# Threshold attention with an MLP behind it: two W transposes moved from TensorE to DMA, the w_out load moved later, one q copy moved up

## The chip, the cores and the metric

The kernel runs on one core of a Trainium2 chip, in one launch. The metric is the device time of that launch in microseconds (us). The kernel before took 495.15 us (median of three runs: 494.38, 495.15 and 495.28).

## The reference

Eight batches of eight heads attend over 576 tokens with 64 dimensions per head. Of each row of scores only those within tau = 0.02 of the row's largest are kept. The attention's output, 4608 tokens of 512 numbers, goes through an MLP with a leaky ReLU.

```python
scores = scale * np.matmul(q, k.transpose(0, 1, 3, 2))          # scale = 1/8
thresh = np.max(scores, axis=-1, keepdims=True) - tau
scores = np.where(scores >= thresh, scores, -1000000000.0)
attn = np.exp(scores - np.max(scores, axis=-1, keepdims=True))
attn = attn / (np.sum(attn, axis=-1, keepdims=True) + 1e-09)
x = np.matmul(attn, v)                                          # heads side by side: 4608 x 512
h = x @ w_in                                                    # 512 x 2048
out = np.maximum(0.01 * h, h) @ w_out                           # 2048 x 512
```

## The kernel before, in words

**Steps.** The work is cut into 144 steps, 18 for each batch. A step takes 128 queries of one pair of heads; the two last steps of a batch take the 64 left-over queries of all heads. Two steps that follow each other (c = 0 and c = 1) make a *pair*: their weights W lie side by side in one tile `w` (`Pair`, line 300). Steps 0 and 1 are the first pair, 4 and 5 the third, 6 and 7 the fourth. The first four pairs give the first 256 tokens of the MLP's input `x`.

**What a step does.** TensorE multiplies q and k (`scores`, L252). The numbers are split in a high and a low half of 16 bits, so a score is three products. VectorE copies the scores out of PSUM, negates them and takes the row's minimum on the way (`copy_min`, L260; two instructions, one per head), then the threshold (`threshold`, L269 in the first 28 steps). ScalarE makes the exponentials (`exps`, L295, L291, L292) one step later, and VectorE the masked weights of the first head (`weights`, L304). The reciprocal of the row sums (`recip`, L310) is written beside the weights by `widen` (L313), so that it is transposed with them.

**The transpose of W.** W must have the keys on the partitions before it can be multiplied with v. There are two ways. `turn_w_pe` (L331, L333) does it in two halves of 10 TensorE transposes for each step, with copies out of PSUM by ScalarE (three of a pair's four) and VectorE (one). `turn_w` (L321) does it for a whole pair with one transposing DMA from the SP queue. `Step.early` (line 34) decides: steps below 8 go by TensorE, two steps behind their scores. All later pairs go by DMA: the pair is noted in `ended` at the end of a step, and in the next step VectorE takes the reciprocal, GpSimd widens it, and SP issues the DMA.

**W times v.** `pv` (L348) follows at a fixed step given by `pv_at`: three steps after the pair's second step for early pairs, five for the others. `evacuate` (L370, VectorE) multiplies by the reciprocal and puts the result into `x`. After the fourth pair of heads `x` is complete, and eight pieces of the first MLP layer (`layer1`, L391) are queued, one of which goes into each later step; the second layer (`layer2`, L407) follows, up to two pieces a step.

**q and k.** They come by DMA from HBM, are scaled and split (`split_*`, L137, L143, L151, mostly on GpSimd) and transposed by TensorE (`turn`, L186) with a copy out of PSUM (L195, L189). The keys of the first batch are in the list `first`; `first[8]` is the last head pair's q, which `scores` first needs in step 6, and `first[9]` the tail's q.

**Order.** There is no scheduler: each engine runs its instructions in the order in which the Python loop writes them, and waits where a tile isn't ready. In a step the order is: loads, `exps` of the step before, `scores`, `copy_min`, the reciprocal of a noted pair, idle products in the first steps, one item of the list for GpSimd (`pool_at`), `threshold`, `widen` and `turn_w` of a noted pair, the rest of `pool_at`, `weights` of the step before, `layer1`, `turn`, `turn_w_pe`, `layer2`, idle products in steps 5 to 10, `pv` and `evacuate`. The SP queue holds the loads of q, k and v, the transposing DMAs and the stores, in the order of the steps. The loads of w_in and w_out are issued by GpSimd (`load_w`, L497 and L500), on a DMA queue of their own, and convert to 16 bits on the way.

**Idle products.** `idle` (L513) multiplies the identity with itself into the PSUM tile of `pv`; nothing reads the result. Since that tile has one buffer, idle products wait for the `evacuate` before them.

**Buffers that matter here.** PSUM: scores two buffers for each head, `pv` one, the "h" tag two. SBUF: `w` three, transposed `wT` four, raw q and k four.

Of the kernel before, what the change touches and what calls it, by code (L numbers as in the profile page):

```python
# [16 lines left out]
class Group:  # L17


    def __init__(self, tokens, where):  # L20
        self.tokens = tokens
        self.where = where
        self.x = None
        self.g = None


class Step:


    def __init__(self, n, b, blk, p, c):  # L30
        self.n, self.b, self.blk, self.p, self.c = n, b, blk, p, c
        self.tail = blk == 2

        self.early = n < 8


@with_exitstack
def kernel(
# [10 lines left out]
    nc = tc.nc  # L49
# [68 lines left out]
    def turned_of(b, which):  # L118
        if (b, which) not in turned:
            turned[b, which] = sb.tile([128, 2, NP, WIDE[which]], FP16, tag=f"{which}T", bufs=2, name=f"{which}T")  # L120
        return turned[b, which]
# [23 lines left out]
    def split_low(key):  # L145

        n = 2 if key[1] == "t" else 4
        m = 2 if key[0] < 2 else n
        src = scaled.pop(key)
        for i in range(0, n, m):  # L150
            nc.gpsimd.tensor_tensor(out=halves[key][:, 1, i : i + m, :, :], in0=src[:, i : i + m, :, :],  # L151
                                    in1=halves[key][:, 0, i : i + m, :, :], op=AX.subtract)
# [18 lines left out]
    def turn(key, copy=None, bank="h"):  # L171
        copy = copy or nc.scalar.copy
        b, p, which = key
        dst, half = turned_of(b, which), halves.pop(key)
        n = 2 if p == "t" else 4
        c0 = 0 if which == "q" else 64
        if p == "t":
            c0 = MAIN if which == "q" else 0
            tp = ps.tile([128, 2, 2, 2, 64], FP16, tag=bank, bufs=2 if bank == "h" else 1, name="tp")
        else:  # L180
            tp = ps.tile([128, 2, 4, 128], FP16, tag="h", bufs=2, name="tp")
        for x in range(2):
            for t in range(n):
                for h in range(2):
                    o = tp[ds(64 * h, 64), x, :, t, :] if p == "t" else tp[ds(64 * h, 64), x, t, :]
                    nc.tensor.transpose(o, half[:, x, t, h, :], ident[:, :])  # L186
        if p == "t":
            src = tp[:, :, :, :, :].rearrange("d x u s p -> d x (u s) p")
            copy(out=dst[:, :, :, ds(c0, 64)], in_=src)  # L189
            if which == "k" and b:  # L190
                nc.gpsimd.tensor_copy(out=dst[:, :, :, 576:640], in_=dst[:, :, :, 0:64])
            elif which == "k":
                nc.vector.tensor_copy(out=dst[:, :, :, 576:640], in_=src)
        else:
            copy(out=dst[:, :, p, ds(c0, 512)], in_=tp[:, :, :, :].rearrange("d x t p -> d x (t p)"))  # L195
# [31 lines left out]
    steps = []  # L227
# [9 lines left out]
    def scores(st):  # L237
        st.sc = [ps.tile([128, 2, 512], FP32, tag="sc", bufs=2, name=f"sc{h}") for h in range(2)]
        for kh in range(2):
            for i, (qx, kx) in enumerate(((0, 0), (1, 0), (0, 1))):  # L240
                for u in range(2 if st.tail else 1):
                    for h in range(2):
                        pair = st.p + u
                        rows = ds(64 * h, 64)
                        key0 = 64 * (1 - h) + 288 * kh
                        if st.tail:
                            lhs = turned[st.b, "q"][rows, qx, pair, MAIN:S]
                            o = st.sc[h][ds(64 * u, 64), kh, 0:288]
                        else:
                            lhs = turned[st.b, "q"][rows, qx, pair, ds(256 * st.blk + 128 * st.c, 128)]  # L250
                            o = st.sc[h][:, kh, 0:288]
                        nc.tensor.matmul(out=o, lhsT=lhs, rhs=turned[st.b, "k"][rows, kx, pair, ds(key0, 288)],  # L252
                                         start=(i == 0), stop=(i == 2), skip_group_check=True)
# [54 lines left out]
    def recip(pr, c, n):  # L308
        pr.rec = sb.tile([128, 2, 2], FP32, tag="rec", bufs=2, name="rec")
        nc.vector.reciprocal(out=pr.rec[:, 0:n, :], in_=pr.sum[:, ds(c, n), :])  # L310

    def widen(pr, c, n, eng=None):
        (eng or nc.gpsimd).tensor_copy(out=pr.w[:, ds(c, n), 9, :].rearrange("q c (h d) -> q c h d", h=2),  # L313
                                     in_=pr.rec[:, 0:n, :].unsqueeze(3).to_broadcast([128, n, 2, 64]))
# [114 lines left out]
    loads_at, turns_at, pool_at = {}, {}, {}  # L429

    def at(d, n, f):
        d.setdefault(n, []).append(f)

    def units(b):
        u = [(b, p, w_) for p in range(NP) for w_ in "kq"]
        return u[:2] + [(b, "t", "k")] + u[2:] + [(b, "t", "q")]
# [3 lines left out]
    for b in range(1, B):  # L440
# [6 lines left out]
        for i, key in enumerate(units(b) if b == 1 else ROWS):  # L447
            n_ = 9 + 3 * i // 2 if b == 1 else base + (5, 7, 9, 9, 11, 13, 15, 17, 19, 21)[i]
            key = (b,) + key[-2:]
# [45 lines left out]
    def load_w(i):  # L495
        if i < 4:
            nc.gpsimd.dma_start(out=w_in16[:, i, :], in_=moe_w_in[ts(i, 128), :])  # L497
        else:
            j = i - 4
            nc.gpsimd.dma_start(out=w_out16[:, ds(4 * j, 4), :],  # L500
                                in_=moe_w_out[ds(512 * j, 512), :].rearrange("(j p) f -> p j f", p=128))


    def split_pool(key):
        split_scale(key)
        split_high(key)
        split_low(key)
# [8 lines left out]
    first = units(0)  # L516
# [8 lines left out]
    for key in first[4:6]:  # L525
        split_high_act(key)
        split_scale(key)
        split_low(key)
    for n_, key in zip((1, 2, 6), first[7:]):
        at(pool_at, n_, lambda key=key: split_pool(key))  # L530
    for i in range(8):
        at(pool_at, i if i < 2 else 1 + i // 2 if i < 6 else i, lambda i=i: load_w(i))
    at(turns_at, 0, lambda: turn(first[3], nc.vector.tensor_copy))
    for n_, key in zip((1, 2, 3, 5, 8), first[5:]):
        at(turns_at, n_, lambda key=key: turn(key, nc.vector.tensor_copy if key[2] == "q" else None))

    N = len(steps)

    pv_at = {s.n + (3 if s.early else 5): s for s in steps if s.c == 1}
    ended = []  # L540
    n = 0
    while n < N + 7 or l1q or l2q or stores:
        for f in loads_at.get(n, []):
            f()
        if 1 <= n <= N:
            exps(steps[n - 1])
        if n < N:
            scores(steps[n])
            turned_now = turn_rows(rows_at[n]) if n in rows_at else None
            copy_min(steps[n])  # L550
            if ended:
                recip(ended[0], 0, 2)
        if n == 0:
            threshold(steps[0])
        if n == 1:
            split_high_act(first[6])
            split_scale(first[6])
            split_low(first[6])
            turn(first[4], nc.vector.tensor_copy)
        if n < 5:  # L560
            idle(8 if n else 16)
        todo = pool_at.get(n, [])
        for f in todo[:1]:
            f()
        if 0 < n < N:
            threshold(steps[n])
        if ended:
            widen(ended[0], 0, 2)
            turn_w(ended.pop())
        if n in rows_at:  # L570
            turned_now(1)
        for f in todo[1:]:
            f()
        if 1 <= n <= N:
            last = steps[n - 1]
            weights(last)
            if last.early:
                recip(last.pair, last.c, 1)
                widen(last.pair, last.c, 1, nc.vector if n < 7 else nc.gpsimd)
            elif last.c == 1 and n < 2 * PERB:  # L580

                ended.append(last.pair)
            elif last.c == 1:
                recip(last.pair, 0, last.pair.n)
                widen(last.pair, 0, last.pair.n)
                turn_w(last.pair)
        if n in rows_at:
            turned_now(0)
        while stores:
            store()  # L590
        if l1q and l1q[0][3] <= n:
            layer1()
        for f in turns_at.get(n, []):
            f()
        if 2 <= n < N + 2 and steps[n - 2].early:
            turn_w_pe(steps[n - 2].pair, steps[n - 2].c)
        for _ in range(2):
            if l2q:
                layer2(n)
        if 5 <= n < 11:  # L600
            idle(8)
        if n in pv_at:
            pv(pv_at[n])
            evacuate(pv_at[n], n)
        n += 1
# [33 lines left out]
```

## Time and profile before

| | us |
|---|---|
| median of three runs | 495.15 |
| the profiled execution | 495.05 |
| its span, from the first to the last instruction | 493.2 |
| TensorE busy | 476.3 |
| ScalarE busy | 431.3 |
| VectorE busy | 408.8 |
| GpSimd busy | 316.3 |
| start of step 6's first `copy_min` | 30.68 |
| start of step 12's first `copy_min` | 50.16 |
| start of step 18's first `copy_min` | 67.94 |

The profiled execution's own time is 1.85 us above its span. A time in the trace counts from the span's start. A convenient mark for "where a step is" is the start of the first of its two L260 instructions on VectorE; the table gives three of them. The engines' busy times overlap, and a share over the whole span hides stages: the first 68 us, in which the MLP has not filled up, look different from the rest. "PEclk" is the TensorE clock that was granted, 1.00 being full. A DMA line gives the packets, the megabytes and the share of time of the 16 DMA engines in the window asked for; q1 is the queue of the DMAs that SP issues, q0 that of GpSimd's.

### The profile page before, as it was taken

What the parts mean: (1) busy time and instruction counts of PE and PEld (TensorE: products, weight loads), DVE (VectorE), ACT (ScalarE), POOL (GpSimd) and SP (SyncE); (2) the same over time, 40 slices, a digit from 0 to 9 for tenths busy, and PEclk for the clock granted to TensorE, in tenths of its full rate; (3) what the DMA queues carried; (4) which work ended last, traced back from release to release, by engine and by line L of the source; (5) the groups of instructions that cost most, each with busy time, mean ns of one, the idle gap of its engine ahead of it and who ended that gap; (6) DMA issues with size and microseconds to landing.
All of it is one profiled execution on the core that took longest, in us unless ns stands there. A gap on an engine that the chain in (4) does not pass through costs nothing.

```text
span 493.2 us, 19697 instructions
## 1 busy us (share of the span) xinstructions
PE 476.3 (97%) x8039; PEld 344.5 (70%) x8039; DVE 408.8 (83%) x1220; ACT 431.3 (87%) x781; POOL 316.3 (64%) x534
## 2 busy tenths in 40 slices
PE   8978989999999999999999999999999999999996
PEld 7656766767677777777777777777777777667883
DVE  4989999998989898989889898989889998888100
ACT  6889988999999999999999999999999999999441
POOL 5996798578766786768766787677767683222000
PEclk9989999999999999999999999999999999999999
DMA  8998799989998998999997898999999988769412
GB/s 247 263 205 144 140 185 186 210 176 192 212 185 160 221 208 196 180 174 234 166 209 162 201 211 198 192 165 224 179 202 163 205 134 169 125 128 146 113 45 66
DMA packets 220443, 87.79 MB, mean 178 GB/s; under 512 B 190656, under 2 KB 217280, under 8 KB 220352
## 3 DMA queue, kind: packets, MB, share of 16 engines
q1 hardware_dynamic: 217120, 82.00, 82.4%
q0 software_dynamic: 2688, 4.19, 4.8%
q8 instruction: 63, 1.03, 0.9%
q10 hardware_dynamic: 544, 0.33, 0.2%
q14 instruction: 28, 0.23, 0.1%
HBM read 36.70 MB, written 9.44 MB: 94 GB/s over the span
## 4 chain that ended last, share of the span: by engine, by line
PE 82%; DVE 4%; ACT 1%; issue 1%; DVEq 0%
PE hp L391 27%; PE o L407 21%; PE sc L252 21%; PE pv L348 7%; PE osc L407 4%; PE tpr L207 3%; DVE s L260 2%; DVE w L304 1%; DVE x L370 0%; PE tp L186 0%; ACT w L292 0%; ACT s L291 0%; ACT e L295 0%; ACT g L393 0%; ACT osb L413 0%
## 5 line engine op out<-in xcount | busy, mean ns | idle before, releaser
L260 DVE TENSOR_SCALAR_CACHE_REDUCE s<-sc 128x576 f32<-128x576 f32 x288 | 206.5, 754 | 34.5 <-PE sc L252 33.0
L252 PE MATMUL sc<-kT,qT 64*128 64x288 f16 (+1 forms) x1920 | 135.1, 285 | 5.2 <-DVE s L260 2.5
L391 PE MATMUL hp<-x,win 128*64 128x256 f16 x2048 | 136.7, 275 | 0.8 <-DVE x L370 0.7
L391 PEld LDWEIGHTS <-win 128*64 128x64 f16 x2560 | 118.5, 109 | 23.8 <-issue 17.8
L407 PE MATMUL o<-wout,g 128*64 128x512 f16 x992 | 127.8, 379 | 0.0
L304 DVE SCALAR_TENSOR_TENSOR w<-s,th,e 128x576 f16<-128x576 f32 x144 | 120.5, 837 | 0.5 <-ACT e L295 0.5
L272 POOL TENSOR_SCALAR th<-mn 128x2 f32<-128x2 f32 x116 | 53.7, 463 | 102.1 <-DVE s L260 79.1
L252 PEld LDWEIGHTS <-qT 64*128 64x128 f16 (+1 forms) x1920 | 76.6, 96 | 59.4 <-issue 42.7
L292 ACT ACTIVATE w<-s,minus_tau 128x576 f16<-128x576 f32 x144 | 111.7, 775 | 5.2
L295 ACT ACTIVATE e<-s,mn 128x576 f16<-128x576 f32 x144 | 110.2, 765 | 2.0 <-DVE s L260 2.0
L291 ACT ACTIVATE s<-s,th 128x576 f32<-128x576 f32 x144 | 110.3, 766 | 1.3 <-POOL th L272 0.9
L393 ACT ACTIVATE g<-hp 128x512 f16<-128x512 f32 x144 | 84.0, 584 | 26.9 <-PE hp L391 26.4
L151 POOL TENSOR_TENSOR half<-scaled,half 128x512 f16<-128x512 f32 (+1 forms) x91 | 90.2, 998 | 2.0
L407 PEld LDWEIGHTS <-g 128*64 128x64 f16 x1152 | 65.2, 110 | 30.0 <-issue 0.5
L348 PE MATMUL pv<-wT,v 128*64 128x256 f16 (+1 forms) x960 | 52.6, 249 | 1.0 <-DMA wT<-w 0.8
L348 PEld LDWEIGHTS <-v 128*64 128x64 f16 x960 | 42.2, 111 | 14.5 <-issue 1.0
L137 POOL TENSOR_SCALAR scaled<-raw 128x512 f32<-128x512 f32 x62 | 44.3, 714 | 5.7 <-DMA raw<-in_k_dram 4.8
L143 POOL CAST half<-scaled 128x512 f16<-128x512 f32 (+1 forms) x74 | 44.3, 599 | 4.5
L313 POOL CAST w<-rec 128x256 f16<-128x256 f32 (+1 forms) x70 | 32.1, 459 | 15.9 <-DVE rec L310 4.6
L106 POOL CAST v<-vraw 128x256 f16<-128x256 f32 x64 | 31.3, 520 | 1.3
L370 DVE TENSOR_TENSOR x<-pv,wT 128x256 f16<-128x256 f32 x64 | 27.0, 422 | 3.8 <-PE pv L348 3.6
L292 ACT ACTIVATION_READ_ACCUMULATOR w<-s,minus_tau 128x1 f32 x144 | 26.9, 187 | 0.0
(53 smaller groups left out, 323.9 us busy)
## 6 DMA issues: line engine op xcount, KB each, us to landing
vraw<-in_v_dram SPq DMA_DIRECT2D x16, 512.0 KB, 5.8
out_dram<-osb SPq DMA_DIRECT2D x16, 512.0 KB, 3.7
raw<-in_k_dram SPq DMA_DIRECT2D x14, 512.0 KB, 4.9
raw<-in_q_dram SPq DMA_DIRECT2D x14, 512.0 KB, 4.9
win<-in_moe_w_in_dram POOLq DMA_DIRECT2D x4, 512.0 KB, 7.1
wout<-in_moe_w_out_dram POOLq DMA_DIRECT2D x4, 512.0 KB, 10.3
wT<-w SPq DMA_TRANSPOSE x68, 5.7
raw<-in_k_dram SPq DMA_DIRECT2D x4, 256.0 KB, 5.3
```

The source lines that it names most:

```text
L151: nc.gpsimd.tensor_tensor(out=halves[key][:, 1, i : i + m, :, :], in0=src[:, i : i + m, :, :], in1=halves[key][:, 0, i : i + m, :, :], op= ...
L252: nc.tensor.matmul(out=o, lhsT=lhs, rhs=turned[st.b, "k"][rows, kx, pair, ds(key0, 288)], start=(i == 0), stop=(i == 2), skip_group_check= ...
L260: nc.vector.tensor_scalar(out=st.s[:, h, :].rearrange("p (a b) -> p a b", a=2), in0=st.sc[h][:, :, 0:288], scalar1=-1.0 / UNIT, scalar2=No ...
L272: nc.gpsimd.tensor_scalar(out=st.th[:, :, 0], in0=st.mn[:, :, 0], scalar1=1.0, scalar2=tau_f, op0=AX.mult, op1=AX.add)
L291: nc.scalar.activation(out=z, in_=z, func=AF.Prelu, bias=st.th[:, h, 0:1], scale=-1.0, alpha=1e20)
L292: nc.scalar.activation(out=st.w[h], in_=z, func=AF.Exp, bias=minus_tau[:, :], scale=1.0, accum_out=st.sum[h])
L295: nc.scalar.activation(out=st.e[:, :], in_=st.s[:, h, :], func=AF.Exp, bias=st.mn[:, h, 0:1], scale=-1.0)
L304: nc.vector.scalar_tensor_tensor(out=st.w[0], in0=st.s[:, 0, :], scalar=st.th[:, 0, 0:1], in1=st.e[:, :], op0=AX.is_le, op1=AX.mult, accum ...
L348: nc.tensor.matmul(out=o, lhsT=v16[st.b % 2][:, 2 * c + u if st.tail else st.p, blk, :], rhs=rhs, start=(i == 0), stop=(i == 4), skip_grou ...
L391: nc.tensor.matmul(out=hp[ds(64 * u2, 64), jj, :], lhsT=w_in16[:, i, ds(128 * j + 64 * u2, 64)], rhs=g.x[:, i, :], start=(i == 0), stop=(i ...
L393: nc.scalar.activation(out=g.g[:, ds(nj * u, nj), :], in_=hp[:, :, :], func=AF.Prelu, bias=0.0, scale=1.0, alpha=0.01)
L407: nc.tensor.matmul(out=g.o[ds(64 * u2, 64), :], lhsT=g.g[:, j, ds(128 * m + 64 * u2, 64)], rhs=w_out16[:, j, :], start=(j == 0), stop=(j = ...
```

## The change

The third and the fourth pair's W go by DMA, with `pv` four steps behind the pair's second step (at steps 9 and 11, where it was at 8 and 10). Their reciprocals are taken for the pair as a whole, by one instruction of VectorE and one `widen` on GpSimd, at steps 7 and 9. The four pieces of w_in stay at steps 0, 1, 2 and 2; the four pieces of w_out move from steps 3, 3, 6 and 7 to steps 8, 9, 10 and 11. The copy of the last head pair's q (and its transposes, which already came right behind the scores on TensorE) is written directly behind `copy_min` of step 5, where it stood at that step's end. The tail's q is split at step 7 and turned at step 10, where it was 6 and 8. The number of idle products stays 96 in steps 0 to 10; in steps 6, 8 and 10 they move from the end of the step to behind the scores.

```diff
-        self.early = n < 8
+        self.early = n < 4
...
-    for n_, key in zip((1, 2, 6), first[7:]):
+    for n_, key in zip((1, 2, 7), first[7:]):
         at(pool_at, n_, lambda key=key: split_pool(key))
     for i in range(8):
-        at(pool_at, i if i < 2 else 1 + i // 2 if i < 6 else i, lambda i=i: load_w(i))
+        at(pool_at, i if i < 2 else 2 if i < 4 else 4 + i, lambda i=i: load_w(i))
...
-    for n_, key in zip((1, 2, 3, 5, 8), first[5:]):
+    for n_, key in zip((1, 2, 3, 10), first[5:8] + first[9:]):
...
-    pv_at = {s.n + (3 if s.early else 5): s for s in steps if s.c == 1}
+    pv_at = {s.n + (3 if s.early else 4 if s.n < 8 else 5): s for s in steps if s.c == 1}
...
             copy_min(steps[n])
             if ended:
                 recip(ended[0], 0, 2)
+            if n == 5:
+                turn(first[8], nc.vector.tensor_copy)
...
-        if n < 5:
+        if n < 11 and (n < 5 or n % 2 == 0):
             idle(8 if n else 16)
...
-                widen(last.pair, last.c, 1, nc.vector if n < 7 else nc.gpsimd)
+                widen(last.pair, last.c, 1, nc.vector)
...
-        if 5 <= n < 11:
+        if 5 <= n < 11 and n % 2:
             idle(8)
```

On the SP queue the two new DMAs stand ahead of loads that were issued early: the third pair's ahead of the second half of the next batch's k and q (`load_main` of steps 8 and 9), the fourth pair's behind these two and ahead of the first v load of the next batch (step 11).

## The prediction

> **What bounds the kernel now.** I read first the page, then the windows by stage, then the timeline around step 6, then the DMA queues in short windows.
>
> From the page:
>
> ```profile
> PE 476.3 (97%) x8039; PEld 344.5 (70%) x8039; DVE 408.8 (83%) x1220; ACT 431.3 (87%) x781; POOL 316.3 (64%) x534
> PEclk9989999999999999999999999999999999999999
> ```
>
> TensorE (PE) is the bound on average. The dip of the clock is a hint that the first tenth is different. Stages, with the columns span length, then busy time and count of PE, weight loads, VectorE (DVE), ScalarE (ACT), GpSimd (POOL), then granted clock, DMA share, GB/s:
>
> ```profile
> 26.04:30.68 4.64, 2.29 (x48) 1.69 (x50) 3.47 (x13) 4.57 (x9) 4.64 (x11) 1.00 0.89 185
> 30.95:34.36 3.41, 3.35 (x38) 2.48 (x34) 3.20 (x12) 3.05 (x7) 3.20 (x6) 0.50 1.00 191
> 30.68:50.16 19.48, 17.50 (x282) 12.85 (x283) 18.14 (x62) 16.91 (x31) 15.32 (x23) 0.91 0.89 161
> 50.16:67.94 17.78, 15.15 (x274) 11.78 (x272) 17.50 (x57) 16.86 (x32) 15.01 (x24) 1.00 0.81 158
> 65.08:68.49 3.41, 1.96 (x28) 1.50 (x29) 3.25 (x11) 2.85 (x7) 3.26 (x6) 1.00 0.56 118
> 67.94:100.00 32.06, 31.35 (x524) 22.26 (x522) 31.18 (x105) 28.26 (x51) 23.89 (x37) 1.00 1.03 198
> 100.00:450.00 350.00, 349.15 (x5962) 249.33 (x5960) 313.57 (x911) 325.87 (x596) 235.80 (x400) 1.00 0.93 184
> ```
>
> From step 18 (67.94) PE is busy 98% and then 99.8%: there the time is PE's work, which the change doesn't shorten. All it touches lies before that. From step 6 to step 18 VectorE is the bound (18.14 of 19.48, 17.50 of 17.78). So the end moves by as much as step 18 moves, plus PE work that changes sides of that point. Before step 6 stands a hole:
>
> ```profile
> 29.00 0.68 DVE L195 COPY qT<-tp 128x1024 f16<-128x1024 f16 x1
> 29.74 0.91 PE L252 MATMUL sc<-kT,qT 64*128 64x288 f16 x12 [2.35 <-DVE qT L195]
> 30.68 0.76 DVE L260 TENSOR_SCALAR_CACHE_REDUCE s<-sc 128x576 f32<-128x576 f32 x1 [1.00 <-PE sc L252]
> 50.27 3.15 SPq L321 DMA_TRANSPOSE wT<-w  x1
> 57.01 0.74 PE L348 MATMUL pv<-wT,v 128*64 128x256 f16 x10 [0.84 <-DMA wT<-w]
> 58.70 0.76 DVE L260 TENSOR_SCALAR_CACHE_REDUCE s<-sc 128x576 f32<-128x576 f32 x1
> ```
>
> Step 6's scores wait 2.35 us for the q copy, VectorE then 1.00 us for the scores, and from 30.95 the clock is halved for 3.41 us (window above). The last three lines are the first transposing DMA: though pv comes five steps behind, PE waits for it. DMA in short windows: both queues at 34 to 37, w_out alone at 38 to 45, that first transpose alone at 51.2 to 54.9, and the landing of eleven transposes:
>
> ```profile
> q0 software_dynamic: 339, 0.35, 70.4%
> q1 hardware_dynamic: 341, 0.35, 42.1%
> ...
> q0 software_dynamic: 1434, 1.43, 123.6%
> ...
> q1 hardware_dynamic: 2592, 0.66, 94.7%
> ...
> wT<-w SPq DMA_TRANSPOSE x1, 6.7
> ...
> DMA to landing us min/median/max: 4.9/5.5/7.2
> ```
>
> So a piece of w_out (0.52 MB) is 2.5 us of all DMA engines, a transpose about 3.1 us, and where GpSimd's queue and SP's both have work, neither goes first: they share packet by packet.
>
> **The change part by part.** Marks are the starts of a step's first L260.
>
> A. The q copy behind step 5's scores. It goes in at 27.50, where the threshold stood, ends at 28.2, and step 6's scores start at 28.25 in place of 29.74. With 0.94 from scores to L260 (29.74 to 30.68) step 6 starts at 29.2. Threshold and weights come 0.7 later and still end by then. Gain 1.5.
>
> B. VectorE's work in steps 6 to 11. A step with nothing but scores, threshold, weights and one pair's reciprocal took 2.53 (47.63 to 50.16). Six make 15.2; three evacuations (start to start 0.33) 1.0; two 128x1024 copies (0.60) 1.2; the tail's q copy 0.3. Sum 17.7 against 19.48: gone are two L333 copies (481 ns), three small reciprocals (168), a widen (227), 1.34 of idle time, and the halved clock, whose cause A removes. PE's 80 transposes (0.72 for 20, 2.9 in all) and ScalarE's six copies (690, 4.1) lie beside VectorE and count nothing; without that cover they would be up to 2.9 more gain. Gain 1.8. Without any wait step 12 would start at 46.9 in place of 50.16.
>
> C. The third pair's transpose. Step 7 starts at 29.2 + 2.53 + 0.33 = 32.1; reciprocal 1.35 later (47.63 to 48.98); from there to SP's issue 1.3 (48.98 to 50.27): 34.7. The landing took 4.9 at best and 6.7 for the kernel's first transpose, which this one now is, with the DMA as empty as there; I take 6.7, 41.4. From pv's start to the next L260 it was 1.69 (57.01 to 58.70): step 10 starts at 43.1, against 40.6 by VectorE alone. Loss 2.5 (0.7 at 4.9). PE stands behind that pv with step 10's scores.
>
> D. The fourth pair's. Its reciprocal is at 38.5 (step 9 at 37.1), but GpSimd has before that widen one scale, one high half and one low half of q, the same of the tail's q, a further scale and the first w_out issue: by the rows 615, 829, two of 747, 398, about 400, 720, 398 and 825 ns, 5.7 after 34.7. Then widen: SP issues at 41.1. In its queue stand two 0.52 MB loads that were issued at 17.5 and 23.4 before and now wait behind C's issue, till 37.9 and 38.5 (1.5 us of DMA each); beside them w_out pieces from about 40.5, one each 2 to 3 us. With equal shares the loads end near 43.3, the transpose needs 2 x 3.1, and lands at 50.2 (0.7 behind its last packet). Step 12 starts at 51.9, against 43.1 + 3.45 + 2.86 = 49.4 without this wait. Loss 2.5. Bounds: 0 (it lands in 5.0 at 46.1, and 47.8 is below 49.4), and 8 if the transpose's 2592 packets alternate one to one with w_out's. I take the equal share, from the row with both queues, 339 against 341.
>
> By the Trainium skill, "DMA: Bandwidth & Descriptors", section on queues, rings and completion order, an engine changes queue only at packet borders, of typically 9 to 17 descriptors; the row of 339 and 341 has pieces of equal size and can't show which of the two counts. By that rule a transpose's pieces of 256 B would hold their half (D = 2.5); by the row read one to one it would be 8.
>
> The moved loads and vector v of batch 1 are not needed before step 12; w_out is needed at step 19 and has 20 us. GpSimd loses two narrow widens and gets two wide ones (292 against 464 ns), which cancels but for 0.3.
>
> E. The clock. In D PE waits from about 45 to 50: longer than the 2.35 that halved it. In a halved window pv took 1.28 for 0.74, scores 1.17 for 0.91 (rows at 32.57 and 33.78). Loss 1.0 (0 if D is 0, 1.5 for a whole window). Steps 7 and 8 now have 0.91 + 0.62 of PE work in 2.5 us, 61%; 57% (1.96 of 3.41 at 65.08) passed without halving, 35% (1.21 of 3.41 at 27.54) did not. The moved idle products cost nothing while PE waits for VectorE anyway; were one late, it would be 0.62.
>
> By the Trainium skill, "TensorE: Matmul & The Clock Gate", the table of why this matters, only idle gaps above about 3 us cool the clock. The gap of 2.35 here did, in a window with 35% of work; by that rule C's gap of about 2 us would be harmless, by the row it could add up to 1.5.
>
> F. `layer1` starts a step later, so one piece (16 products, 0.99) leaves the part that VectorE bounds and joins the part that PE bounds. 0 to 1.0; VectorE is 97% busy in 67.94 to 100, so half: 0.5.
>
> Sum: -1.5 - 1.8 + 2.5 + 2.5 + 1.0 + 0.5 = +3.2. The profiled execution, 495.05 (0.1 below the median of the runs, so no correction), becomes 498.3.
>
> **The rivals.** R1, the transposes land in time. For it: from 33 to 36 the DMA now has nothing, 4.9 us is a common landing, and C then costs 0.7 and D and E nothing: -3.3 + 0.7 + 0.5 = -2.1, 492.9. Against it: the one transpose of before that met an empty DMA is the 6.7. It decides when C's transpose lands before 40 and D's before 47.5.
>
> R2, the first lands late and the second is hidden behind it (D and E 0): -3.3 + 2.5 + 0.5 = -0.3, 494.8, no difference. For it: C itself gives D time. Against: GpSimd's 5.7 us and the loads in front are in no row faster.
>
> R3, w_out gets a packet for each of the transpose's: D = 8, E = 1.5: 504.3. For it: 339 to 341. Against: nothing shows it for 256-byte pieces.
>
> That the change does nothing at all I leave out: the 2.35 us hole goes in any case, since PE's transposes of that q end at 26.27 and only VectorE's order kept the copy back.
>
> **How the numbers follow.** Forecast 0.50, R1 0.28, R2 0.12, R3 0.10. What a measurement of this kernel can tell from no change is about 0.2%, 1 us. Faster 0.28, same 0.12, slower 0.60. Predicted 498.3. The range takes in R1 with another 0.4 for F at nothing, and reaches up to half way into R3: 492.5 to 502.0; the forecast's own is 496 to 502.
>
> **What would show it.** A: no PE wait for qT before step 6, step 6 at about 29.2. B: steps 7 and 8 of about 2.5. C: a PE wait of pv for the DMA near 39 to 41. D: another near 45 to 50, the fourth pair's landing over 8 us after its issue, both DMA queues busy together. E: a row of granted clock 0.50 behind that wait, none at 31. F: PE full from step 18 or 19 on. The prediction is wrong if the DMA serves the transpose ahead of w_out, if GpSimd reaches its widen earlier, or if steps 12 to 18 give back what was lost.

## The result

The changed kernel takes 508.83 us (median of four executions, 507.87 to 511.14). The kernel before took 494.76 beside it (median of four, 494.27 to 495.28). The ratio is 1.029, with a 95% interval of 1.025 to 1.033: slower by 14.1 us, where 3.2 were forecast. The sign was right and the size was not. The profiled execution of the changed kernel is the slowest of the four, 511.14 with a span of 508.9, so 2.3 us of what its trace shows is spread between executions of this kernel.

From the profile's page of the changed kernel: the busy shares, the slices with the granted clock, the group of `pv`, and the line of w_out in the table of DMA issues (the last number is us from issue to landing).

```profile
PE 477.6 (94%) x7959; PEld 343.9 (68%) x7959; DVE 407.9 (80%) x1214; ACT 428.6 (84%) x775; POOL 316.1 (62%) x534
PE   8874198999999999999999999999999999999996
PEclk9987589999999999999999999999999999999999
...
L348 PE MATMUL pv<-wT,v 128*64 128x256 f16 (+1 forms) x960 | 52.6, 249 | 17.5 <-DMA wT<-w 17.3
...
wout<-in_moe_w_out_dram POOLq DMA_DIRECT2D x4, 512.0 KB, 14.9
```

The engines' busy times have hardly moved (TensorE 477.6 for 476.3). What is new is one hole: the fifth slice, 51 to 64 us, where PE is busy a tenth and the clock is at half. `pv` waits 17.3 us for transposed weights, against 0.8 before, and a piece of w_out lands 14.9 us after its issue (median of the four; 10.3 before).

The timeline of TensorE shows the three waits that the prediction spoke of (start, duration, then in brackets the idle time before and what ended it):

```profile
28.01 0.91 PE L252 MATMUL sc<-kT,qT 64*128 64x288 f16 x12 [0.74 <-DVE qT L195]
...
41.33 0.74 PE L348 MATMUL pv<-wT,v 128*64 128x256 f16 x10 [0.89 <-DMA wT<-w]
...
61.84 1.28 PE L348 MATMUL pv<-wT,v 128*64 128x256 f16 x10 [16.43 <-DMA wT<-w]
```

And the timeline of the SP queue, with the time that each issue kept SP (the transposing DMAs are those of the third, fourth and fifth pair):

```profile
34.42 3.21 SPq L321 DMA_TRANSPOSE wT<-w  x1
37.69 0.57 SPq L78 DMA_DIRECT2D raw<-in_k_dram  x1
38.31 0.59 SPq L78 DMA_DIRECT2D raw<-in_q_dram  x1
41.40 9.55 SPq L321 DMA_TRANSPOSE wT<-w  x1
...
51.74 13.34 SPq L321 DMA_TRANSPOSE wT<-w  x1
```

Up to 43 us the forecast holds closely in its marks: q's wait is 0.74 us where it was 2.35 (none was forecast), the first transpose is issued at 34.42 (forecast 34.7), its pv starts at 41.33 (forecast 41.4), step 10 begins at 43.02 (forecast 43.1). What was not forecast is a halved clock from 33.7 to 40.6. The fourth pair's transpose is issued at 41.40 (forecast 41.1), and then it all parts: landing takes 20.4 us where 9.1 were forecast, its pv waits 16.43 us, step 12 begins at 64.78 in place of 51.9.

What the DMA did in that time, in four short windows of the same trace (packets, MB, share of the 16 engines' time): the third pair's transpose alone, 36 to 38; w_out alone, 44 to 45, while the fourth pair's transpose has been issued for 3 us; both, 47 to 51; and both, 51 to 58.

```profile
q1 hardware_dynamic: 1685, 0.43, 115.6%
...
q0 software_dynamic: 173, 0.18, 120.3%
...
q1 hardware_dynamic: 435, 0.11, 88.3%
q0 software_dynamic: 187, 0.19, 55.7%
...
q0 software_dynamic: 940, 0.94, 89.7%
q1 hardware_dynamic: 987, 0.25, 38.2%
```

Three things are to be seen.

- In 44 to 45 the transpose's queue q1 has no packet. The last packets of the two loads of k and q in front of it came by 43.8; its own first ones come near 45.4, 4 us after the issue. The third pair's, with no w_out beside it, came 1.3 us after its issue, at 35.7.
- From 51 to 58 the packets go one to one, 940 against 987, though one of w_out carries 1 KB and one of the transpose 256 B. In 47 to 51 they do not: 187 against 435.
- Together they are slower than one after the other. In 47 to 51 the transpose moved 435 packets in 4 us, 109 per us, where alone it moved 843; w_out moved 47 per us, where before it moved 205 alone. Over 45 to 62 the two queues moved 1667 and 2845 packets; of the latter 2592 are the transpose's and some 250 those of a load of v behind it. At 205 and 843 packets per us the first two are 8.1 and 3.1 us of work, and the load of v about 0.7 (at 385 per us, which loads of k and q reached without w_out): 12 us of work, an estimate, in 17 us.

SP is held for 9.55 us by that issue, where the first four issues of the kernel before took 3.1 to 3.8, and for 13.34 by the fifth pair's behind it.

### The profile page after: what moved, and what is told of

The parts are those of the page before. It is cut to its first block, busy times and chain, and to the rows that moved or that the text cites. A ratio compares the mean times of both kernels' runs of the same rounds, so it can differ in the third digit from the quotient of the medians.

```text
span 508.9 us, 19530 instructions
## 1 busy us (share of the span) xinstructions
PE 477.6 (94%) x7959; PEld 343.9 (68%) x7959; DVE 407.9 (80%) x1214; ACT 428.6 (84%) x775; POOL 316.1 (62%) x534
## 4 chain that ended last, share of the span: by engine, by line
PE 79%; DVE 4%; ACT 1%; issue 1%; POOL 0%; DVEq 0%; POOLq 0%
PE hp L391 26%; PE o L407 20%; PE sc L252 20%; PE pv L348 7%; PE osc L407 3%; PE tpr L207 3%; DVE s L260 2%; DVE w L304 1%; ACT w L292 1%; DVE x L370 0%; ACT s L291 0%; ACT e L295 0%; DVE th L269 0%; PE tp L186 0%; POOL th L272 0%
## 5 line engine op out<-in xcount | busy, mean ns | idle before, releaser
L252 PE MATMUL sc<-kT,qT 64*128 64x288 f16 (+1 forms) x1920 | 138.1, 288 | 4.0 <-DVE s L260 2.9
L391 PEld LDWEIGHTS <-win 128*64 128x64 f16 x2560 | 118.9, 110 | 23.6 <-issue 17.3
L304 DVE SCALAR_TENSOR_TENSOR w<-s,th,e 128x576 f16<-128x576 f32 x144 | 121.2, 842 | 0.5 <-ACT e L295 0.5
L393 ACT ACTIVATE g<-hp 128x512 f16<-128x512 f32 x144 | 83.9, 583 | 43.3 <-PE hp L391 43.0
L272 POOL TENSOR_SCALAR th<-mn 128x2 f32<-128x2 f32 x116 | 52.0, 449 | 103.3 <-DVE s L260 77.4
L151 POOL TENSOR_TENSOR half<-scaled,half 128x512 f16<-128x512 f32 (+1 forms) x91 | 91.0, 1006 | 2.0
L348 PE MATMUL pv<-wT,v 128*64 128x256 f16 (+1 forms) x960 | 52.6, 249 | 17.5 <-DMA wT<-w 17.3
L137 POOL TENSOR_SCALAR scaled<-raw 128x512 f32<-128x512 f32 x62 | 44.6, 719 | 5.6 <-DMA raw<-in_k_dram 4.7
L143 POOL CAST half<-scaled 128x512 f16<-128x512 f32 (+1 forms) x74 | 42.7, 577 | 4.5
L313 POOL CAST w<-rec 128x256 f16<-128x256 f32 x70 | 32.7, 467 | 16.0 <-DVE rec L310 5.9
## 6 DMA issues: line engine op xcount, KB each, us to landing
wout<-in_moe_w_out_dram POOLq DMA_DIRECT2D x4, 512.0 KB, 14.9
```

Of the source, the lines that this page charges most:

```text
L272: nc.gpsimd.tensor_scalar(out=st.th[:, :, 0], in0=st.mn[:, :, 0], scalar1=1.0, scalar2=tau_f, op0=AX.mult, op1=AX.add)
L304: nc.vector.scalar_tensor_tensor(out=st.w[0], in0=st.s[:, 0, :], scalar=st.th[:, 0, 0:1], in1=st.e[:, :], op0=AX.is_le, op1=AX.mult, accum ...
L348: nc.tensor.matmul(out=o, lhsT=v16[st.b % 2][:, 2 * c + u if st.tail else st.p, blk, :], rhs=rhs, start=(i == 0), stop=(i == 4), skip_grou ...
L391: nc.tensor.matmul(out=hp[ds(64 * u2, 64), jj, :], lhsT=w_in16[:, i, ds(128 * j + 64 * u2, 64)], rhs=g.x[:, i, :], start=(i == 0), stop=(i ...
L393: nc.scalar.activation(out=g.g[:, ds(nj * u, nj), :], in_=hp[:, :, :], func=AF.Prelu, bias=0.0, scale=1.0, alpha=0.01)
```

## The experiments

The theory formed after the result: the loss is the meeting of w_out's packets with a transposing DMA, and nothing else of the change costs anything. The rivals: the loss hangs on where w_out was put; the transposes are slow by themselves; the other edits (q's copy, the tail's q, idle products) cost part of it. The runs with only an edit of the kernel before test the gain that was forecast for A. Each ratio is taken against the kernel before as it ran beside; its medians there went from 494.76 to 496.29 us, so experiments are compared with each other by their ratios where a microsecond matters.

**w_out back at its old steps, all else changed.**

```diff
-        at(pool_at, i if i < 2 else 2 if i < 4 else 4 + i, lambda i=i: load_w(i))
+        at(pool_at, i if i < 2 else 1 + i // 2 if i < 6 else i, lambda i=i: load_w(i))
```

> The changed kernel with w_out's four loads back at steps 3, 3, 6 and 7. Theory T1 (a transposing DMA and a w_out load that run at the same time slow each other down): now the third pair's transpose, issued near 34.4, falls into the time in which w_out is loaded (33 to 45 in the kernel before), so it lands 10 to 20 us after its issue in place of 6.9, pv of step 9 waits 6 us or more, the fourth pair's lands sooner than its 20.4; time 500 to 510. Theory T2 (the fourth pair's transpose is late for its place in SP's queue, behind two loads of q and k, and for GpSimd's late widen): the third lands in 6.9 and the fourth in about 20 as in the changed kernel; time 507 to 510.

Measured: 507.58 us, ratio 1.0245 (1.0225 to 1.0264), nearly the whole loss. SP's issue of the third pair's transpose, and TensorE's wait for it:

```profile
34.94 10.34 SPq L321 DMA_TRANSPOSE wT<-w  x1
...
52.28 1.28 PE L348 MATMUL pv<-wT,v 128*64 128x256 f16 x10 [12.24 <-DMA wT<-w]
```

w_out is now issued from 27.9 to 38.6 and meets the third pair's transpose, which lands in 17.3 us; the fourth pair's lands in 9.1, and no pv waits for it. Its DMA shows the same signs. In 35 to 39.5 the transpose, issued at 34.94, is held back to 9 packets beside 812, with no load in front of it:

```profile
q0 software_dynamic: 812, 0.80, 117.4%
q1 hardware_dynamic: 9, 0.00, 0.4%
```

So at each of these two places w_out hits a transpose, the fourth pair's at one and the third's at the other.

**No w_out at all.** The four loads are left out, and the second layer multiplies with columns of w_in.

```diff
-                                 rhs=w_out16[:, j, :], start=(j == 0), stop=(j == 15), skip_group_check=True)
+                                 rhs=w_in16[:, j % 4, 0:512], start=(j == 0), stop=(j == 15), skip_group_check=True)
...
-    for i in range(8):
+    for i in range(4):
```

> The changed kernel without any load of w_out; the second MLP layer multiplies with columns of w_in in its place, so the output isn't the reference's. All queue places, widens and instructions of the engines stay. T1: the fourth pair's transpose, issued near 41.4, lands in 5 to 7 us, pv of step 11 waits at most 1 us, step 12 starts at 49 to 50; time 493 to 496. T2: the landing stays near 20 us and the time near 508.

Measured: 494.83 us, ratio 0.9999 (0.9986 to 1.0013). The two transposes, and the two waits for them:

```profile
34.78 3.20 SPq L321 DMA_TRANSPOSE wT<-w  x1
...
41.17 3.74 SPq L321 DMA_TRANSPOSE wT<-w  x1
...
41.60 0.74 PE L348 MATMUL pv<-wT,v 128*64 128x256 f16 x10 [2.16 <-DMA wT<-w]
...
46.62 0.74 PE L348 MATMUL pv<-wT,v 128*64 128x256 f16 x10 [0.94 <-DMA wT<-w]
```

The transposes land in 6.8 and 5.4 us, though the same k and q loads still stand in SP's queue before the second; its first packets come near 42.8, 1.6 us after the issue and not 4. GpSimd loses its four issues of w_out (0.8 us each) too, but the second transpose is issued only 0.23 us earlier for it. The w_out meeting is 508.83 - 494.83 = 14.0 us; what is left of the change, as it stands, is worth nothing (within 0.7 us).

**A quarter of w_out.** As the run before, with one of the four pieces loaded, at step 8 (`range(5)` in the last line above; the second layer as there).

> The changed kernel with one of the four pieces of w_out (at step 8); the second layer multiplies with columns of w_in, so the output isn't the reference's. If the DMA only shares packet by packet (the prediction's R3), one piece delays the fourth pair's transpose by no more than the 2.5 us that the piece takes alone: landing within 8 us, time 496.5 to 498. If the cost is as in the changed kernel in proportion (14.0 us for four pieces), 3.5 us: 498 to 499. If meeting w_out at all is what costs (a start held back or a slow phase that one piece triggers), more than half of the 14 us: over 502.

Measured: 498.22 us (496.53 to 500.36), ratio 1.0057 (1.0035 to 1.0078). The fourth pair's transpose held SP for 6.57 us, landed in 8.7, and its pv waited 3.16. Against the kernel before that is a loss of 2.8 us (1.7 to 3.9), where the run without w_out lost nothing. A quarter of 14.0 is 3.5, and the piece is 2.5 us of DMA alone; the interval holds both, so that the loss goes with the number of pieces is not shown, only that one piece does not cost half of it. This trace shows the start that is held back, and hardly any slowing: in 44 to 46 w_out's queue moved 387 packets, close to its full pace, and the transpose's 42; in 47 to 49, when the piece was through, SP's queue moved 2052. In this run the loss needs no more than the piece's own time.

**Only w_out moved, in the kernel before.** The diff is the first one read backwards, in the kernel before.

> The kernel before with only w_out's loads moved to steps 8 to 11; the third and fourth pair stay with TensorE. T1: the loads now run until past 50 and meet the first transposes of the kernel before (issued at 50.3 and 55.7); the first lands 10 to 15 us after its issue in place of 6.7, pv waits 4 to 9 us in place of 0.8; time 498 to 504. T2: no difference, 494 to 496.

Measured: 499.48 us, ratio 1.0079 (1.0055 to 1.0103). Here the fifth pair's transpose, the first of that kernel, meets the last of w_out, and lands in 9.7 us:

```profile
49.60 6.18 SPq L321 DMA_TRANSPOSE wT<-w  x1
...
59.32 0.74 PE L348 MATMUL pv<-wT,v 128*64 128x256 f16 x10 [3.44 <-DMA wT<-w]
```

So the move costs some 4 us even where no pair's transpose is moved: a wait of 3.44 us for 0.84, and a halved clock behind it (from 60.2 to 63.6). It is the same meeting with another transpose: in each run with a loss of 2.5 us or more so far, w_out and a transpose were in flight at one time.

**Without w_out, and pv one step later.** As the second run, with pv of the two pairs five steps behind.

```diff
-    pv_at = {s.n + (3 if s.early else 4 if s.n < 8 else 5): s for s in steps if s.c == 1}
+    pv_at = {s.n + (3 if s.early else 5): s for s in steps if s.c == 1}
```

> The kernel without loads of w_out, and the two pv at five steps (10 and 12) in place of four. The prediction's step C says that pv of step 9 waits for the transpose and holds step 10's scores behind it: in the run without w_out PE waited 2.16 and 0.94. With pv a step later both waits go, step 10 starts near 41, step 12 near 47.5; one more piece of the first MLP layer moves behind step 18 (0.5): 493 to 494. Rival: the halved clock of steps 7 and 8 held step 10 anyway: within 0.3 of 494.8.

Measured: 494.22 us, ratio 0.9971 (0.9958 to 0.9984). No pv waits for the DMA any more; step 10 starts at 41.67 (43.29 in the run with pv at four), step 12 at 48.09 (49.15). Against the kernel before it is 1.4 us faster (0.8 to 2.1), where the run with pv at four came out even (0.7 faster to 0.6 slower): without w_out and with this pv the change would have a small gain.

**All weights earlier, pv five steps behind.** Can w_out be out of the way in time? This is the whole computation again.

```diff
-        at(pool_at, i if i < 2 else 2 if i < 4 else 4 + i, lambda i=i: load_w(i))
+        at(pool_at, (0, 1, 1, 1, 2, 2, 3, 3)[i], lambda i=i: load_w(i))
```

> The changed kernel whole, with pv of the third and fourth pair five steps behind (as in the run before it) and all eight pieces of the weights issued earlier: at steps 0, 1, 1, 1, 2, 2, 3, 3. The eight pieces are some 20 us of DMA at 205 packets a us (0.52 MB each, 2.5 us), and before they began at 17; so w_out can be done at 38 to 40 at best, in place of about 46. Theory (a transpose is held back and slowed only while w_out's packets are in flight): the third pair's transpose, issued near 34.8, is held back to about 38 to 39 and lands near 42 to 43; pv, due near 41, waits 1 to 2 us, the fourth waits nothing: 494.5 to 496.5. Rival 1: the earlier loads delay the first steps' k and q, and step 5 starts 1 us or more later than at 26: 496 to 498. Rival 2: the collision of the third pair costs what it cost with w_out at its old steps, about 12 us: 505 or more.

Measured: 498.59 us against 496.29 beside it, ratio 1.0054 (1.0031 to 1.0076), above what the theory gave. All pieces are issued by 29.5, but they keep the DMA till about 44. The third pair's transpose was issued at 35.78, held SP 8.65 us and landed in 10.7:

```profile
46.54 1.28 PE L348 MATMUL pv<-wT,v 128*64 128x256 f16 x10 [5.02 <-DMA wT<-w]
```

The wait is 5.02 us in place of 1 to 2. At 40, w_out's expected end at the latest, 262 of its packets were left, 1.3 us of DMA alone; beside the transpose they took until 44. So the meeting was shortened and not avoided.

**The same, with only the fourth pair by DMA** (`self.early = n < 6`).

> As the run with the earlier weight loads, but only the fourth pair's W goes by DMA; the third pair's stays on TensorE. Theory: the fourth pair's transpose is issued near 41, when w_out has landed, lands in 5 to 7 us at 46 to 48, and pv of step 12 (near 47.5 to 48.5) doesn't wait for it; the third pair's copies and widens stay, so that half of the gain of the run without w_out and with pv a step later is left: 494 to 495.5, which can't be told from the kernel before. Rival 1: the earlier loads delay k and q of the first steps, 496 to 498. Rival 2: w_out's rest still meets the transpose: PE waits 3 us or more for wT, 498 or more.

Measured: 495.69 us against 496.29 beside it, ratio 0.9994 (0.9978 to 1.0011). The transpose is issued at 42.01, when w_out is all but done (43 packets are left), holds SP 3.33 us and lands in 6.7; no pv waits for it. So a transposing DMA at step 9 is harmless once w_out is past, and then it is worth nothing that can be measured.

**Only q's copy moved up, in the kernel before.**

```diff
-    for n_, key in zip((1, 2, 3, 5, 8), first[5:]):
+    for n_, key in zip((1, 2, 3, 8), first[5:8] + first[9:]):
...
+            if n == 5:
+                turn(first[8], nc.vector.tensor_copy)
```

> The kernel before with only the copy of the last head pair's q moved behind step 5's copy_min. By step A of the prediction step 6 starts at 29.2 in place of 30.68, and the halved clock at 31 to 34 goes: 1.5 to 2.5 us faster, 492.5 to 493.5. Rival: the lead is eaten by a later wait (GpSimd's widen for steps 6 and 7, or the clock halving elsewhere): 494.5 to 495.

Measured: 495.67 us, ratio 0.9994 (0.9979 to 1.0009): no gain, where 492.5 to 493.5 was expected. In the profile the hole before step 6 is gone, and so is the halved clock. Step 5 takes 3.89 us in place of 4.64. But steps 6 to 8 take 11.58 in place of 10.82, and so all of it is lost again. Part of it is a wait for GpSimd's widen, which is 1.53 us here and 0.81 in the kernel before:

```profile
38.56 0.25 PE L331 MATMUL wp<-ident,w 128*64 128x128 f16 x2 [1.53 <-POOL w L313]
```

**The same with every widen of the early pairs on VectorE,** to remove this wait.

```diff
-                widen(last.pair, last.c, 1, nc.vector if n < 7 else nc.gpsimd)
+                widen(last.pair, last.c, 1, nc.vector)
```

> The kernel with only the q copy early, and the widens of steps 6 and 7 on VectorE in place of GpSimd. In the run with the q copy alone PE's transposes of step 6's W waited 1.53 us for that widen on GpSimd, which was busy without a break. If GpSimd is what ate the lead, that wait goes, VectorE pays 0.23 twice, step 12 starts about 1 us earlier (48.6 to 49.0): 493.2 to 494.2, against about 494.9 before. If something else holds step 8, the time stays at 494.5 to 495.5.

Measured: 495.52 us against 495.38, ratio 1.0006 (0.9995 to 1.0017): no gain where 493.2 to 494.2 was expected, so removing the wait for GpSimd wins nothing. It is gone, and one of 1.76 us for a copy of VectorE stands in its place. VectorE's masked weights (L304) took 1.54 and 1.86 us in steps 7 and 8, where the kernel before has 0.88 and 1.08 and the shortest take 0.81. First the two lines of this run, then the two of the kernel before:

```profile
34.47 1.54 DVE L304 SCALAR_TENSOR_TENSOR w<-s,th,e 128x576 f16<-128x576 f32 x1
38.02 1.86 DVE L304 SCALAR_TENSOR_TENSOR w<-s,th,e 128x576 f16<-128x576 f32 x1
```

```profile
36.55 0.88 DVE L304 SCALAR_TENSOR_TENSOR w<-s,th,e 128x576 f16<-128x576 f32 x1
39.16 1.08 DVE L304 SCALAR_TENSOR_TENSOR w<-s,th,e 128x576 f16<-128x576 f32 x1
```

While they ran, GpSimd ran its subtractions (L151) and scalings (L137): two L151 from 34.08 to 35.38, an L137 from 35.35 that took 1.13 in place of 0.61. The two L304 are 1.4 us longer together than in the kernel before (1.3 in the run with only q's copy moved, which has 1.54 and 1.75), more than the 0.76 that was lost; that GpSimd is the cause was not tested by itself, and it can't be all: the L304 of the kernel before at 39.16 ran beside two L151 as well (38.93 to 40.76) and took 1.08. A slowing by GpSimd agrees with the Trainium skill, "GPSIMD Engine Reference", section on specifications, by which the two engines share their interfaces to SBUF and contend when VectorE reads two operands from there, as L304 does.

**The same with the tail's q later** (split at step 7, turned at step 10, as in the changed kernel), to take GpSimd's and VectorE's work out of steps 6 to 8.

> The same, and the tail's q split at step 7 and turned at step 10 as in the changed kernel (1.9 us of GpSimd moved one step later). If GpSimd's order around steps 6 and 7 still costs something: another 0.2 to 0.6 us, 492.8 to 494.0. If not, as the run before.

Measured: 496.61 us, ratio 1.0023 (1.001 to 1.0036), slower than the kernel before. L304 took 1.31 at 36.51 for 1.54 to 1.86 before, but TensorE waited 1.43 us for a widen of VectorE, and the clock was at half from 36 to 42. This one is not explained further.

## Why the prediction was wrong

**A, q's copy (-1.5): nearly right in size, worth nothing by itself.** Step 5 takes 3.51 us in place of 4.64, a gain of 1.13, and step 6 starts at 29.42 where 29.2 was said: the L304 behind the copy took 1.32 us for 0.81, and step 6's first `copy_min` stood behind it. But in the kernel before the edit alone gives no time: the 0.75 that it won in step 5 was lost again, 0.76, in the three steps behind. The prediction took a lead won in step 5 as one that is kept. In the changed kernel steps 6 to 8 take 8.97 us for 10.82, and the lead is kept; that this is because the transposes and widens are gone there is argued, not tested by itself.

**B, VectorE's work in steps 6 to 11 (-1.8): right.** The run in which no pv waits for the DMA (w_out left out, pv five steps behind) takes 18.0 us from step 6 to step 12 (30.07 to 48.09), where 17.7 was worked out. The single steps came out otherwise than said: 6 and 7 take 3.0 each in the changed kernel, since L304 took 1.17 and 1.05 us in them and not the 0.81 of a quiet step, and the `copy_min` behind step 7 waited 0.38 for scores at the halved clock.

**C, the third pair's transpose (+2.5): right, a little smaller.** pv starts at 41.33 for 41.4, and from step 6 to step 10 it is 13.6 us for 13.9. Without w_out this stretch takes 13.5 with pv four steps behind (29.78 to 43.29) and 11.6 with five (30.07 to 41.67): C is 1.9.

**D, the fourth pair's transpose (+2.5): this term failed.** Its way there was right: GpSimd's order put the widen at 40.99, SP issued at 41.40. The duration was wrong. In the changed kernel's trace its pv starts at 61.84, and at 46.62 without w_out: 15.2 us, of which up to 2.3 is this execution's distance from the median. Three steps of the working made it 2.5. (Its 3.1 us for a transpose alone was a little low, too: the row of 2592 packets, 94.7% of 3.7 us, gives 3.5.)

- It let the transpose begin behind the two k and q loads in front, which end near 43.3. They ended by 43.8, but then came 1.6 us in which w_out ran alone.
- It took equal shares, as the row of 339 against 341 packets seemed to allow. Equal they were in 51 to 58, but by packets, 940 to 987, with four times the bytes on w_out's side; R3 had that, at a chance of 0.10.
- It took the total pace of the DMA as constant. So did every rival, R3's bound of 8 included, and it was not: 12 us of work took 17.

**E, the halved clock (+1.0): right in size.** From step 12 to step 18 the profiled execution took 18.34 us, and 17.65 without w_out; pv to step 12 took 2.94 for 2.53. Together 1.1. That is in part luck: behind this wait the halved clock lasted for 6.2 us of work (last row below), where the working reckoned with one window of 3.41 at most. But the other part, that 61% of TensorE's work keeps steps 7 and 8 at the full clock, was wrong. The windows of the changed kernel (busy time of PE first, granted clock third from the end):

```profile
30.49:33.91 3.42, 1.89 (x23) 1.27 (x22) 3.39 (x13) 3.39 (x7) 2.10 (x3) 0.97 0.68 137
33.91:37.32 3.41, 3.33 (x24) 1.95 (x25) 3.00 (x12) 2.73 (x6) 3.11 (x6) 0.50 0.52 99
37.32:40.73 3.41, 3.12 (x33) 2.09 (x29) 2.79 (x12) 2.83 (x5) 3.38 (x5) 0.53 0.88 187
...
61.84:68.04 6.20, 6.20 (x58) 4.02 (x58) 3.11 (x10) 1.48 (x3) 0.47 (x1) 0.51 1.05 192
```

A window with 1.89 of 3.42 (55%) was followed by a halved one; the 57% on which the claim rested was not. The steps came out longer than 2.5, so the share was below the 61%. But the share alone does not decide: the clock changed at 33.7, and the 3.41 us that end there have 60%; in the run without w_out a window with 51% (1.73 of 3.38, 37.72 to 41.10) was followed by the full clock; and here a halved window with 98% was followed by a second halved one. What decides at such loads stays open. How much it cost here was not measured by itself; C came out no larger than forecast.

**F (+0.5): right.** Without w_out step 18 comes 1.14 earlier than before (66.80 for 67.94) and the span is shorter by 0.5: 0.6 is lost behind that point. With pv five steps behind it is 2.1 and 1.0 of span: 1.1 is lost. Each is from one profiled execution.

**The rivals.** R1 (both land in time, 492.9) never came about: even with w_out left out and pv five steps behind the gain is 1.4 and not 2.1, since A gave 0.4 less, B 0.3 less, and F took up to 1.1, while C took nothing. R2 (494.8) is what the kernel takes without w_out, 494.83, but by its absence and not by C's cover. R3 had the sharing packet for packet and the sign of the miss: with D = 8 and E = 1.5 it said 504.3, 4.5 below the median. So of the 14.1 us, 14.0 are the meeting; the rest of the change, on which most of the working was spent, adds to nothing (within 0.7 us).

## What to carry to other kernels

Before a transposing DMA is put where TensorE waits for it, look what else the DMA engines hold at that time, and from which queue: a bulk load on another queue can hold its first packet back for microseconds and then take the pace from both, and sharing by packets favours the queue with the larger ones. Cost such a meeting from a window in which just these two kinds overlap; where the trace has none, the upper bound must leave room for a total that falls below either alone (75 GB/s in 47 to 51, where the transpose alone moved 216 and w_out alone 177). And a hole that is closed on one engine is only a gain if the engines behind it can use the lead.

## What the runs showed of the hardware

- A transposing DMA on SP's queue and casting loads on GpSimd's disturb each other by more than their sum: 12 us of work took 17, and four pieces that are 10 us of DMA alone cost 14.0 us of time. One piece cost 2.8 (1.7 to 3.9), which its own 2.5 us can explain. With four pieces landing went from 5.4 to 20.4 us, and SP's issue from 3.74 to 9.55. The transpose's first packets came 4 us after the issue in place of 1.6; in the run with w_out at its old steps there were 9 packets in the first 4.6 us.
- The Trainium skill, "DMA: Bandwidth & Descriptors", section on queues, rings and completion order, has an engine drain a packet of typically 9 to 17 descriptors from one queue before it turns to the next. The prediction drew from it that the transpose's small pieces hold their half, which the section, speaking of packets and not of bytes, doesn't say. What was measured, 0.25 MB against 0.94 in 51 to 58, doesn't bear that inference out; and nothing in the section lets the total fall. Why it falls is open: no run here tells whether it is the issue, the small packets or the conversion.
- The clock was halved at 33.7 in the changed kernel, behind 3.41 us in which TensorE worked 60% and its longest idle time was 0.73 us. The Trainium skill, "TensorE: Matmul & The Clock Gate", the table of why this matters, asks for no idle gaps above about 3 us between bursts of products; here, and at the gap of 2.35 us in the kernel before, the clock fell without one, so in this case's traces keeping to that is not enough. That *only* such gaps lower it is the prediction's wording. No share of work in a window separates the cases either, as said above under E.
